# One half batch's x turned by VectorE and a scratch in DRAM instead of TensorE, with new order lists, in a fused attention and MLP kernel

## The chip, the cores and the metric

The kernel runs on one core of a Trainium2 chip. The metric is the time of one execution on the device in microseconds; the median of several runs counts. The engines are named as in the profile: PE (TensorE, matrix products), DVE (VectorE), ACT (ScalarE), POOL (GpSimd) and SP (SyncE, which issues most DMAs).

## The reference, cut to what matters

Attention over chosen chunks of keys for 4 batches, 8 heads, 768 positions and 64 dimensions a head, and then an MLP with ELU over all 3072 positions.

```python
top_chunks = np.argsort(ub, axis=-1)[..., -top_k:]     # 6 of 24 chunks of 32 keys, causal
scores = scale * np.matmul(q, k.transpose(0, 1, 3, 2))
...
scores = np.where(sel & causal, scores, -1e9)
attn = softmax(scores)
x = matmul(attn, v)            # to [3072, 512], heads side by side
h = x @ w_in                   # [3072, 2048]
g = np.where(h > 0, h, np.exp(np.minimum(h, 0)) - 1)
out = g @ w_out                # [3072, 512]
```

## The kernel before, in words

**Units.** A "pair" u (0 to 15) is two heads of a batch; batch b has pairs 4b to 4b+3. Each pair's queries are worked on in two halves of 384 positions (hf 0 and 1). "12,0" below is pair 12, first half; "half 3,0" is the MLP of batch 3's first half.

**Attention of a half pair** (`pair_attend`). PE makes the scores (line 863) in pieces, ACT takes their exponentials (L890), PE multiplies them with V (L922, six groups of matmuls, one for each of two heads and three blocks of 128 queries, "P·V" below), DVE takes the reciprocal of the sums (L935) and scales (L938), which gives the tile `on`: 128 positions on the partitions, three blocks of 128 features along the row. The MLP needs x with the features on the partitions, so PE turns `on` with three transposes into PSUM (L947), and ACT copies the result into `xT` (L950). An `xT` holds both halves of one pair, and one `up` of the MLP reads the `xT` of all four pairs of its batch.

**MLP of a half batch** (`mlp`). `up` (L972) makes 128 rows of h at a time (256 for batch 3, in a two-bank tile), ACT and DVE apply ELU (L982, L987, L990, L1000, L1005, L1011, L1016) and give `gT`; `down` (L1032) multiplies `gT` with `w_out`, in three row tiles of four parts; ACT copies to `osb` (L1041), and SP stores 128 rows of out (L1046).

**Buffers.** `caps` gives the number of buffers of each class. For what follows: `on` 3, `osb` 3, `f` 13 (loads of k, q, v, and the exponentials of ELU), `H` 3 (PSUM banks for `up` of batches 0 to 2, out of four single banks shared by all small PSUM tiles). A new tile of a class takes over a buffer and waits until all that read the old tile are done with it.

**What sets the order.** The operations are collected first with `add`, which numbers them in the order of the calls. For each engine `QUEUE` lists those numbers in the order in which that engine is to run them. `Plan.order` goes through the lists with its own estimates of durations and of the DMA rings and decides, by the time at which it believes a buffer to be free, which buffer a tile gets; it never changes the order of an engine. An engine runs its list strictly in order, so a waiting operation holds up all behind it. `free=[...]` names the buffers that an operation gives back, in the planner's reckoning after its `dur` plus `lat`. A `fetch` is a number of DMAs that SP issues, with 0.533 us of issue for each, `lat=0.0`, and a `DMA` operation that stands for the landing.

Of the kernel before, what the change touches and what calls it, by code (L numbers as in the profile page):

```python
# [14 lines left out]
BF16 = mybir.dt.bfloat16  # L15
# [58 lines left out]
    ],  # L74
    "POOL": [
# [10 lines left out]
    ],  # L86
    "ACT": [
# [20 lines left out]
    ],  # L108
# [5 lines left out]
    ],  # L114
# [43 lines left out]
class Plan:  # L158
# [71 lines left out]
    SHARE = {128: 1.0, 256: 0.35, 512: 0.3, 768: 0.3, 1024: 0.3, 2048: 0.5}  # L230
    HEAVY = 0.088
    RAMP = 240.0
    PAUSE = ((0.0, 2.28), (17.2, 17.8), (21.6, 22.4), (30.5, 31.3))
    LANDED = 0.75

    def served(self, rings, t, until):
# [877 lines left out]
```

## Time and profile before

| | |
|---|---|
| median of three runs | 273.88 us (272.23 to 274.41) |
| the profiled execution's own time | 273.46 us |
| its span, first to last instruction | 271.8 us, granted clock 0.998 |
| PE busy | 258.6 us, 95% |
| DVE, ACT, POOL busy | 206.8, 200.0, 118.3 us |
| the first load lands, PE starts | 4.2 us after the start |
| last matmul to the end of the span | 3.4 us |

How to read it: the busy share of an engine is an average over stages with different limits, and matmuls overlap in the profile, so their mean duration is more than what each adds; distances between starts show that. "A <- B" in a list of waits means that A's engine stood idle until B was done. In the timeline a row gives the start, the length from the first start to the last end of so many like instructions, engine, line, operation, what is written and read, and in brackets the idle time before. "SPq" is SP's queue of DMA issues.

### The profile page before, as it was taken

To read this page: it belongs to the slowest core of one execution; us is meant where nothing else is said; L and a number is where in the kernel's file an instruction comes from. 1 tells how busy PE (TensorE), PEld (TensorE's weight loads), DVE (VectorE), ACT (ScalarE), POOL (GpSimd) and SP (SyncE) were. 2 spreads that over 40 slices of the span, in tenths; PEclk is the share of its full clock that TensorE was granted. 3 is DMA by queue.
4 is the path that set the end of the run, shared out by engine and by line. 5 is a ranking of instruction groups with operands and counts; after the bars stand their busy time and mean duration, and the time that the engine had idled before them with its cause. 6 is when DMAs were issued, how large, how long until landed. Compare 5 with 4: busy or idle time off the path is not lost.

```text
span 271.8 us, 6603 instructions
## 1 busy us (share of the span) xinstructions
PE 258.6 (95%) x2456; PEld 160.0 (59%) x2456; DVE 206.8 (76%) x532; ACT 200.0 (74%) x375; POOL 118.3 (44%) x209
## 2 busy tenths in 40 slices
PE   3898899999999899999999999999999999999995
PEld 3787566655565455655565556665666655555544
DVE  5698979899999979889998867786666875137530
ACT  3899999846996589989899478977898744243512
POOL 3577783155876696870874055544330000000000
PEclk9999999999999999999999999999999999999999
DMA  7997999999999995999931010000210101110113
GB/s 218 266 211 124 205 216 214 164 176 151 148 203 130 192 169 115 139 156 201 240 103 41 1 58 22 0 2 3 76 41 1 41 2 39 39 41 0 65 53 116
DMA packets 112624, 29.79 MB, mean 110 GB/s; under 512 B 101200, under 2 KB 109648, under 8 KB 112592
## 3 DMA queue, kind: packets, MB, share of 16 engines
q1 hardware_dynamic: 107280, 24.39, 48.5%
q0 software_dynamic: 4224, 4.19, 9.3%
q10 hardware_dynamic: 1088, 0.79, 0.9%
q8 instruction: 19, 0.31, 0.5%
q14 instruction: 13, 0.11, 0.1%
HBM read 27.26 MB, written 6.29 MB: 123 GB/s over the span
## 4 chain that ended last, share of the span: by engine, by line
PE 78%; ACT 7%; DVE 6%; DMA 6%; issue 1%; SPq 1%; POOL 0%; DVEq 0%; ACTq 0%; POOLq 0%
PE psH L972 20%; PE psM L1032 20%; PE psS L863 10%; PE psS L972 8%; PE psMT L1032 8%; PE psO L922 6%; ACT pt L890 3%; DMA w_in_sb<-in_moe_w_in_dram 3%; PE psS L771 2%; ACT lhs L695 2%; PE psT L947 2%; DMA out_dram<-osb 1%; PE psMT L685 1%; DMA gT<-in_k_dram 1%; PE psH L685 1%
## 5 line engine op out<-in xcount | busy, mean ns | idle before, releaser
L890 ACT ACTIVATE pt<-psS 128x768 bf16<-128x768 f32 (+1 forms) x120 | 89.8, 781 | 11.3 <-PE psS L863 6.7
L972 PE MATMUL psH<-xT,w_in_sb 128*128 128x384 bf16 x384 | 73.7, 326 | 0.5 <-DMA w_in_sb<-in_moe_w_in_dram 0.4
L1032 PE MATMUL psM<-w_out_sb,gT 128*128 128x512 bf16 x288 | 72.1, 379 | 0.0
L972 PEld LDWEIGHTS <-w_in_sb 128*128 128x128 bf16 x512 | 47.7, 97 | 33.1 <-issue 1.3
L863 PE MATMUL psS<-rhs,lhs 88*128 88x384 bf16 (+4 forms) x304 | 54.6, 283 | 2.8 <-ACT pt L890 2.8
L1032 PEld LDWEIGHTS <-gT 128*128 128x128 bf16 x400 | 37.3, 97 | 33.0 <-DVE gT L1016 0.5
L982 ACT ACTIVATE f<-psH 128x384 f32<-128x384 f32 x96 | 47.0, 506 | 7.0 <-PE psH L972 6.1
L909 POOL TENSOR_SCALAR_AFFINE_SELECT pt<-pt 128x512 bf16<-128x512 bf16 (+1 forms) x48 | 24.7, 522 | 61.6 <-ACT pt L890 58.1
L1011 DVE SCALAR_TENSOR_TENSOR t<-f,psH 128x384 bf16<-128x384 f32 x56 | 30.1, 547 | 12.9 <-ACT f L982 12.4
L863 PEld LDWEIGHTS <-lhs 88*128 88x128 bf16 x304 | 27.4, 98 | 17.8 <-issue 3.0
L737 POOL CAST rhs<-f 64x768 bf16<-64x768 f32 (+1 forms) x40 | 27.7, 698 | 20.4 <-DVE f L622 8.6
L821 POOL COPY rhs<-selt 24x576 bf16<-24x576 bf16 (+2 forms) x40 | 22.7, 566 | 24.2 <-DVE selt L810 22.5
L922 PEld LDWEIGHTS <-pt 128*128 128x128 bf16 x672 | 28.3, 98 | 7.4 <-issue 1.0
L1016 DVE SCALAR_TENSOR_TENSOR gT<-psH,t 128x384 bf16<-128x384 f32 x56 | 30.5, 551 | 1.1
L922 PE MATMUL psO<-vext,pt 128*128 128x65 bf16 x672 | 31.1, 194 | 0.1
L950 ACT ACTIVATE xT<-psT 128x384 bf16<-128x384 bf16 x32 | 15.6, 497 | 11.9 <-PE psT L947 11.9
L972 PE MATMUL psS<-xT,w_in_sb 128*128 128x384 bf16 x128 | 22.9, 326 | 0.0
L982 ACT ACTIVATE f<-psS 128x768 f32<-128x768 f32 x16 | 13.0, 811 | 13.5 <-PE psS L972 13.5
L990 DVE SCALAR_TENSOR_TENSOR gT<-f,psH 128x384 bf16<-128x384 f32 x40 | 21.3, 541 | 2.0 <-ACT psH L987 1.3
L1032 PE MATMUL psMT<-w_out_sb,gT 128*128 128x512 bf16 (+1 forms) x112 | 22.6, 349 | 0.0
L737 POOL CAST lhs<-f 64x768 bf16<-64x768 f32 x24 | 19.7, 823 | 6.4 <-DVE f L604 5.5
L987 ACT ACTIVATE psH<-psH 128x384 f32<-128x384 f32 x40 | 20.2, 512 | 0.0
(55 smaller groups left out, 278.9 us busy)
## 6 DMA issues: line engine op xcount, KB each, us to landing
out_dram<-osb SPq DMA_DIRECT2D x23, 256.0 KB, 2.2
f<-in_k_dram SPq DMA_DIRECT2D x48, 96.0 KB, 3.9
f<-in_q_dram SPq DMA_DIRECT2D x48, 96.0 KB, 3.8
f<-in_v_dram SPq DMA_DIRECT2D x24, 192.0 KB, 3.9
w_in_sb<-in_moe_w_in_dram POOLq DMA_DIRECT2D x4, 512.0 KB, 9.2
w_out_sb<-in_moe_w_out_dram POOLq DMA_DIRECT2D x4, 512.0 KB, 14.7
gT<-in_k_dram SPq DMA_DIRECT2D x8, 192.0 KB, 4.3
gT<-in_v_dram SPq DMA_DIRECT2D x12, 128.0 KB, 4.2
```

The source lines that it names most:

```text
L737: nc.gpsimd.tensor_copy(out=o, in_=i)
L821: eng.tensor_copy(out=dst.rearrange("c h (i two x) -> c h i two x", two=2, x=32)[:, :, :, odd, :], in_=tiles[st][r0:r0 + NCH, c0:c0 + n].r ...
L863: nc.tensor.matmul(p_s[:, hd, pc:pc + w], lhsT=tiles[pt_["kb"]][0:64 + NCH, hd, 128 * kb:128 * kb + 128], rhs=tiles[pt_["qb"]][0:64 + NCH, ...
L890: lambda bs=bs, pt=pt, wtot=wtot, lo=lo, at=at: nc.scalar.activation(out=tiles[pt][:, :, lo:lo + wtot], in_=tiles[bs[0]][:, :, at:at + wto ...
L909: nc.gpsimd.affine_select(out=a, in_=a, compare_op=AOT.is_ge, fill=0.0, base=0, pattern=pat, channel_multiplier=-1)
L922: nc.tensor.matmul(po[:, hd, qi, :], lhsT=tiles[pt][:, hd, off:off + 128], rhs=tiles[pt_["vx"]][:, 6 * hd + kb, :], start=(kb == 0), stop= ...
L972: nc.tensor.matmul(ph, lhsT=w_in_sb[:, kk, f0:f0 + 128], rhs=tiles[XT[4 * b + kk]][:, c0:c0 + HALF], start=(kk == 0), stop=(kk == NKK - 1))
L982: lambda e=e, view=view: nc.scalar.activation(out=halves(e)[:, 0:step], in_=view(), func=AF.Exp),
L990: lambda e=e, view=view, fc=fc, gt=gt: nc.vector.scalar_tensor_tensor(out=tiles[gt][:, fc:fc + step, :], in0=halves(e)[:, 0:step], scalar= ...
L1011: lambda e=e, t=t, view=view: nc.vector.scalar_tensor_tensor(out=tiles[t][:, 0:step], in0=halves(e)[:, 0:step], scalar=1.0, in1=view(), op ...
L1016: lambda t=t, view=view, fc=fc, gt=gt: nc.vector.scalar_tensor_tensor(out=tiles[gt][:, fc:fc + step, :], in0=view(), scalar=0.0, in1=tiles ...
L1032: nc.tensor.matmul(pm, lhsT=tiles[gt][:, fc, 128 * tt:128 * tt + 128], rhs=w_out_sb[:, fc, x0:x1], start=(fc == 0), stop=(fc == NFC - 1))
```

## The change

For batch 3's first half alone (`TURN = ((3, 0),)`), that is for 12,0, 13,0, 14,0 and 15,0:

- The three transposes on PE, the PSUM bank for them and ACT's copy go. Instead DVE transposes `on` in blocks of 32x32 into a second buffer of class `on`; SP issues four stores of it into a scratch in DRAM (128 pieces of 192 bytes each), waits until they have landed, and issues one load of 128 rows of 768 bytes into `xT`. The operations in the lists are called the block transpose, the stores (PUT) and the load back (GET) below. The positions of the half then stand in another order along `xT`.
- Therefore out of that half is stored with two DMAs for a row tile instead of one, each to its own rows.
- Each of the four half pairs has 7 operations in place of 4, so there are 1671 instead of 1659, and numbers from 1405 on are shifted.
- Constants of the planner are changed, and all lists are new.

```diff
+    PAUSE = ((0.0, 2.28), (17.2, 18.0), (21.8, 22.6), (30.5, 31.3), (53.0, 54.0), (61.0, 62.0), (67.0, 68.2), ...
-        add("DMA", 0.0, -20.0, lambda: None, reads=[("asked", i)], writes=[name], lat=plan.LANDED)
+        add("DMA", 0.0, -20.0, lambda: None, reads=[("asked", i)], writes=[name], lat=plan.LANDED + (0.8 if i else 0.3))
...
+    TURN = ((3, 0),)
...
+            if (u // 4, hf) in TURN:
+                xb, = new("on")
+                there = dram.tile([P, HALF], BF16, name=f"xd{u}_{hf}")
...
+                def blocks():
+                    nc.vector.transpose(out=flat(xb).rearrange("p (j t x) -> p t j x", j=4, x=32),
+                                        in_=flat(on).rearrange("p (t j x) -> p t j x", j=4, x=32))
+                def put():
+                    for i in range(4):
+                        nc.sync.dma_start(out=there[:, 96 * i:96 * i + 96].rearrange("(j a) y -> a j y", j=4),
+                                          in_=flat(xb)[32 * i:32 * i + 32].rearrange("a (j y) -> a j y", j=4))
+                add("DVE", dve(HALF), pr, blocks, reads=[on], writes=[xb], alloc=[xb], free=[on])
+                fetch(4, 128, 192, pr, put, [("put", u, hf)], more=[xb], free=[xb])
+                fetch(1, 128, 768, pr,
+                      lambda: nc.sync.dma_start(out=tiles[xt_h][:, HALF * hf:HALF * hf + HALF], in_=there[:, :]),
+                      [(xt_h, hf)], more=[("put", u, hf)], alloc=[] if hf else [xt_h])
+                return
...
+                    if (b, hf) in TURN:
+                        def put(osb=osb, row=b * S + HALF * hf, tt=tt, x0=x0, x1=x1):
...
+                                nc.sync.dma_start(out=o4[i, t0:t0 + n],
+                                                  in_=tiles[osb][p0:p0 + 32 * n, 0:x1 - x0])
+                        add("SP", 1.066, pr, put, reads=[osb], free=[osb], move=(0, 1.08, 0.533, 2, 64, 4 * w))
```

The new lists around this place, with the numbers put into names (`sc` a score piece of two matmuls of 384 columns or as much, `up 2,1:4` the rows 128*4 on of half 2,1, `down 2,1 t1.0` row tile 1, part 0):

```
PE, before, 498 entries ahead of up 3,0:0; the last of them:
  P·V 15,0 (with transposes 14,0 in between), down 2,0 t2.3, sc 15,1, transposes 15,0, up 2,1:4, up 2,1:12, up 3,0:0
PE, after, also 498 entries ahead:
  P·V 14,0, sc 14,1, sc 14,1, transposes 12,1, down 2,0 t2.0, down 2,0 t2.1, P·V 15,0,
  up 2,1:4, down 2,0 t2.2, sc 14,1, up 2,1:14, down 2,0 t2.3, sc 15,1, up 2,1:3, sc 15,1,
  up 2,1:12, up 2,1:5, sc 14,1, up 2,1:13, down 2,1 t1.0, up 3,0:0, up 3,0:2, ...
  (transposes 13,1 follow 24 entries after up 3,0:0)
DVE, after:
  normalize 13,0, block transpose 13,0, ELU 2,1:2, ELU 2,1:9, normalize 13,1, ELU 2,1:10,
  normalize 14,0, block transpose 14,0, normalize 15,0, block transpose 15,0,
  ELU 2,1:4 (two operations), :11 (two), :14 (two), :3 (two), :12 (two), :5 (one), ELU 3,0:0, ...
SP, after:
  PUT 12, out 1,1 t2, GET 12, out 2,0 t0, PUT 13, PUT 14, out 2,0 t1, PUT 15, GET 14, GET 13, GET 15, out 2,0 t2, ...
```

Elsewhere the lists differ all along: the middle entry of a list is moved by 2 places (PE 3), nine entries in ten by no more than 5 to 9. At the start SP asks for the first halves' k of all four pairs one after the other, and POOL asks for the fourth piece of `w_in` behind a cast of pair 4, the V cast of 0,1 and a mask of chunks, where it stood ahead of these three. In SP's list out 0,0 t2 stands ahead of the k load of pair 11 instead of behind it.

More of the change, by code (lines that the diff above doesn't have):

```diff
@@ L227, in clocked @@
         return dur if warm else dur + dur
-    ALONE = {128: 0.0138, 256: 0.0188, 512: 0.036, 768: 0.0368, 1024: 0.055, 2048: 0.085}
-    SHARE = {128: 1.0, 256: 0.35, 512: 0.3, 768: 0.3, 1024: 0.3, 2048: 0.5}
+    ALONE = {128: 0.0138, 192: 0.0166, 256: 0.0188, 512: 0.036, 768: 0.0376, 1024: 0.055, 2048: 0.085}
+    SHARE = {128: 1.0, 192: 0.6, 256: 0.35, 512: 0.3, 768: 0.3, 1024: 0.3, 2048: 0.5}
     HEAVY = 0.088
     RAMP = 240.0
-    PAUSE = ((0.0, 2.28), (17.2, 17.8), (21.6, 22.4), (30.5, 31.3))
+    PAUSE = ((0.0, 2.28), (17.2, 18.0), (21.8, 22.6), (30.5, 31.3), (53.0, 54.0), (61.0, 62.0), (67.0, 68.2), (80.6, 81.6), (85.4, 86.2), (98.0, 99.0), (108.0, 109.0), (117.0, 118.0))
     LANDED = 0.75
@@ L257, in served @@
             if heavy and heavy[0][4]:
-                heavy[0][1] += self.RAMP
+                heavy[0][0] = t + self.RAMP * self.HEAVY / 16
                 heavy[0][4] = 0
+                continue
             rate = {}
@@ L269, in served @@
                     rate[e] = 16 / cyc
+            if not heavy and len(heads) == 2:
+                (e0, h0), (e1, h1) = heads
+                c0, c1 = self.ALONE[h0[2]], self.ALONE[h1[2]]
+                if max(c0, c1) > 1.5 * min(c0, c1):
+                    rate[e0] = 16 / c0 * (0.75 if c0 < c1 else 0.25)
+                    rate[e1] = 16 / c1 * (0.75 if c1 < c0 else 0.25)
             first = min(heads, key=lambda x: x[1][1] / rate[x[0]])
@@ L409 @@
     work = ctx.enter_context(tc.tile_pool(name="work", bufs=1))
+    dram = ctx.enter_context(tc.tile_pool(name="dram", bufs=1, space=bass.MemoryType.DRAM))
     psum = ctx.enter_context(tc.tile_pool(name="psum", bufs=1, space=bass.MemoryType.PSUM))
@@ L574, in fetch @@
         add(eng, 0.533 * starts, pr, f, reads=more, writes=[w] + writes, lat=0.0,
-            move=(0 if eng == "SP" else 1, 1.08 if eng == "SP" else 1.3, 0.533, starts, packets, size), **kw)
+            move=(0 if eng == "SP" else 1, 1.08 if eng == "SP" else 1.75, 0.533, starts, packets, size), **kw)
         add("DMA", 0.0, pr, lambda: None, reads=[w], writes=writes, lat=plan.LANDED)
+    TURN = ((3, 0),)
     PAIR = {}
@@ L941, in pair_attend, with flat @@
                 reads=o_all + [rc], writes=[on], alloc=[on], free=bo + [rc])
+            if (u // 4, hf) in TURN:
+                xb, = new("on")
+                there = dram.tile([P, HALF], BF16, name=f"xd{u}_{hf}")
+                def flat(h):
+                    return tiles[h].rearrange("p q h d -> p (q h d)")
+                def blocks():
[11 more added lines that the diff above has]
+                return
             bx = bank("T")
@@ L1044, in mlp @@
                     row = b * S + HALF * hf + 128 * tt
+                    if (b, hf) in TURN:
+                        def put(osb=osb, row=b * S + HALF * hf, tt=tt, x0=x0, x1=x1):
+                            o4 = out[row:row + HALF, x0:x1].rearrange("(t i r) y -> i t r y", i=4, r=32)
+                            for p0, i, t0, n in (((0, 0, 0, 3), (96, 1, 0, 1)), ((0, 1, 1, 2), (64, 2, 0, 2)),
+                                                 ((0, 2, 2, 1), (32, 3, 0, 3)))[tt]:
+                                nc.sync.dma_start(out=o4[i, t0:t0 + n],
+                                                  in_=tiles[osb][p0:p0 + 32 * n, 0:x1 - x0])
+                        add("SP", 1.066, pr, put, reads=[osb], free=[osb], move=(0, 1.08, 0.533, 2, 64, 4 * w))
+                        continue
                     add("SP", 0.533, pr,
```

171 rows, old and new, of the table QUEUE are left out of this document.

## Prediction

> **What bounds the kernel now.** I read the page first (shares, slices, chain), then the busy time by stretch, then who TensorE (PE) waited for, and last the timeline around the place of the change.
>
> ```profile
> span 271.8 us, 6603 instructions
> PE 258.6 (95%) x2456; PEld 160.0 (59%) x2456; DVE 206.8 (76%) x532; ACT 200.0 (74%) x375; POOL 118.3 (44%) x209
> PE   3898899999999899999999999999999999999995
> GB/s 218 266 211 124 205 216 214 164 176 151 148 203 130 192 169 115 139 156 201 240 103 41 1 58 22 0 2 3 76 41 1 41 2 39 39 41 0 65 53 116
> ```
>
> ```profile
> core 0: us, PE busy (x) PEld busy (x) DVE busy (x) ACT busy (x) POOL busy (x), PEclk, DMA share, GB/s
> 122.00:258.00 136.00, 136.00 (x1131) 80.08 (x1129) 95.73 (x216) 96.51 (x175) 37.83 (x63) 1.00 0.19 51
> 176.00:212.00 36.00, 36.00 (x370) 22.61 (x369) 23.68 (x67) 30.14 (x55) 11.81 (x21) 1.00 0.06 23
> ```
>
> ```profile
> engine line waited for: us in total, times, longest us
> PE psH L685 <- DMA gT<-in_k_dram: 4.2, 1, 4.2
> PE psS L863 <- ACT pt L890: 2.8, 5, 1.4
> PE psH L685 <- ACT qa L721: 1.1, 2, 0.9
> PE psT L947 <- DVE on L938: 0.8, 1, 0.8
> PE psH L972 <- DMA w_in_sb<-in_moe_w_in_dram: 0.4, 1, 0.4
> ```
>
> PE is the bound. From 122 to 258 us it is never idle, and the change lies inside that stretch: work taken off PE there shortens the kernel, and every wait put there lengthens it one for one. Outside it PE loses 4.2 us before the first load and 5.1 us (2.8 + 1.1 + 0.8 + 0.4) to single waits. VectorE (DVE) and ScalarE (ACT) are two thirds and five sixths busy around 176 to 212, and the transfers are at 23 GB/s there, against over 200 early on.
>
> **The change part by part.** (1) PE loses the twelve transposes of line 947 for pairs 12 to 15, first half; ACT loses four copies of line 950; DVE gains four block transposes.
>
> ```profile
> L947 PE MATMUL psT<-ident_b,on 128*128 128x128 bf16 x96 | 10.3, 219 | 0.9 <-DVE on L938 0.8
> L950 ACT ACTIVATE xT<-psT 128x384 bf16<-128x384 bf16 x32 | 15.6, 497 | 11.9 <-PE psT L947 11.9
> L810 DVE STREAM_TRANSPOSE selt<-selv 128x384 bf16<-128x384 bf16 x2 | 1.2, 578 | 0.0
> ```
>
> ```profile
> 208.16 0.35 PE L922 MATMUL psO<-vext,pt 128*128 128x65 bf16 x6
> 208.35 1.03 PE L1032 MATMUL psM<-w_out_sb,gT 128*128 128x512 bf16 x4
> 208.67 0.19 DVE L935 RECIPROCAL rc<-psO 128x6 f32<-128x6 f32 x1
> 208.89 0.56 DVE L938 TENSOR_TENSOR on<-psO,rc 128x384 bf16<-128x384 f32 x1
> 209.22 0.49 PE L863 MATMUL psS<-rhs,lhs 88*128 88x384 bf16 x2
> 209.54 0.33 PE L947 MATMUL psT<-ident_b,on 128*128 128x128 bf16 x3
> 209.71 1.46 PE L972 MATMUL psH<-xT,w_in_sb 128*128 128x384 bf16 x8
> 211.01 0.65 PE L972 MATMUL psS<-xT,w_in_sb 128*128 128x384 bf16 x3
> ```
>
> The mean of 219 ns is no price, because matmuls overlap. The distance from one start to the next is: three transposes 209.54 to 209.71, 0.17 us; an `up` of the earlier half 0.65 (two from 209.71 to 211.01); a `down` 0.87; a score piece 0.32; six P·V matmuls 0.19, so a pair's twelve take 0.38. Four times 0.17 is **-0.67 us** on PE's path. The ACT copies gain nothing, ACT not being the bound there. DVE's four block transposes (the same shape and type as line 810's row, 0.58 us each, 2.3 us) hide beside PE, DVE being busy 23.68 of 36 us; without that cover they would cost up to 2.3.
>
> (2) The round trip. Sixteen small stores (192-byte pieces) and four loads go through SP, which sits idle there, and the stores of out for half 3,0 go from three to six, three more issues of about 0.5 us beside this row:
>
> ```profile
> 189.32 79.95 SPq L1046 DMA_DIRECT2D out_dram<-osb  x14
> ...
> 0.81 1.97 SPq L663 DMA_DIRECT2D gT<-in_k_dram  x4
> ...
> DMA to landing us min/median/max: 2.0/2.0/2.7
> out_dram<-osb SPq DMA_DIRECT2D x2, 128.0 KB, 1.7
> ...
> DMA to landing us min/median/max: 2.5/3.8/17.8
> ```
>
> (Issues from 186 us on, four issues in a row, the landing of line 1046's stores between 186 and 212 us, the two 128 KB stores, the landing of line 592's 96 KB loads.) Four issues take 1.97 us, so the fourth starts 1.5 after the first. A landing x lies between 1.7 (the smallest store; ours have 24 KB) and 2.5 (the quickest load); I take 1.7 for a store, 2.0 for the load back.
>
> I put the new lists into names and time them with the distances above, from T, the end of pair 14's P·V. Pair 15's P·V ends at T+2.9 (two score pieces 0.64, the three transposes of 12,1 0.17, two `down` 1.74, its own 0.38). Then come six `up` 3.90, three `down` 2.61 and four score pieces 1.28 before the first `up` of half 3,0: due at T+10.7. It needs all four pairs. Normalizing ends 1.1 after P·V (208.35 to 209.45), the block transpose 0.6 later: pair 14's at T+1.7. Its stores are issued at once and land at T+3.2+x.
>
> Here is what I expect to go wrong. The class `on` has three buffers. When pair 15's block transpose is to start, one holds 13,1 (its PE transposes stand behind `up` of half 3,0), one holds pair 15's own normalized tile, and one pair 14's turned tile, which four stores are still reading. The planner frees that after its four issues (2.13 us, `lat=0.0`); the chip must wait for the landing, as ACT does for a store of out in the row at 93.39 below. So pair 15's block transpose starts at T+3.2+x instead of T+4.0: it waits x-0.8, 0.9 us at x=1.7. Behind it in DVE's list stand the eleven operations for `up` 4, 11, 14, 3, 12 and 5 of half 2,1.
>
> ```profile
> L1011 DVE SCALAR_TENSOR_TENSOR t<-f,psH 128x384 bf16<-128x384 f32 x56 | 30.1, 547 | 12.9 <-ACT f L982 12.4
> L1016 DVE SCALAR_TENSOR_TENSOR gT<-psH,t 128x384 bf16<-128x384 f32 x56 | 30.5, 551 | 1.1
> ```
>
> Each pair of them takes 1.1 us and frees one of three `H` banks; `up` 3, 12, 5 and 13 each need one. Followed through in turn, `up` 13 starts some 0.15 less late than the block transpose did: PE loses **0.8 us**. The transfers alone give T+3.8+x for the end of the block transpose, T+5.3+2x for its stores, T+5.3+3x for the load back, against T+10.7: a stall of 3x-5.4, nothing at 1.7, 0.6 at 2.0, 2.1 at 2.5. These two waits overlap. Ends of the term: 0 (the planner's own spacing, 0.15 in hand at the buffer) and 2.1; I stay near the store rows, since nothing else moves then. Pair 14's normalizing takes the buffer of pair 13's turned tile in the same way, but its P·V comes 4.9 us after pair 13's: 0.3 us in hand at x=2.
>
> The Trainium skill ("DMA: Bandwidth & Descriptors", section "Anatomy of one DMA — SWDGE (gpsimd) path") gives a DMA of GpSimd's path a fixed cost of about 2.0 us, most of it the receipt of the write, and warns that it is longest towards HBM. If SP's path is alike, x would be 2.0 for stores too, the wait 1.2 and the loss 1.05, so the sum would end 0.25 higher; the trace has 1.7 for 128 KB and 2.0 for 256 KB, and I keep the rows.
>
> (3) The lists made anew. The planner's constants emit nothing; they only move buffers. One place in the lists can be priced, here from the chain of waits and the timeline:
>
> ```profile
> 87.76 0.52 SPq L592
> ...
> 88.33 0.82 SPq L592
> ...
> 89.19 0.59 SPq L592
> ...
> 89.82 3.55 DMA out_dram<-osb
> ```
>
> ```profile
> 93.39 0.60 ACT L1041 ACTIVATE osb<-psM 128x512 f32<-128x512 f32 x1 [1.74 <-DMA out_dram<-osb]
> 94.74 0.49 PE L863 MATMUL psS<-rhs,lhs 88*128 88x384 bf16 x2 [1.36 <-ACT pt L890]
> 95.44 0.48 PE L863 MATMUL psS<-rhs,lhs 88*128 88x384 bf16 x2 [0.22 <-ACT pt L890]
> ```
>
> ACT waits 1.74 us for a store of out that frees its buffer, and PE 1.58 us for ACT. In SP's new list that store stands ahead of pair 11's k load, whose four issues it stood behind: it can go about 2 us earlier (89.82 less 87.76), more than the 1.74, so the wait could go whole. But what holds SP there are free `f` buffers, and ACT's list around it is another too. Ends 0 and -1.6; I take half, **-0.8 us**. The other 3.5 us of single waits (5.1 less 1.6) lie before 36 us and around 75, where the new lists load the first halves' k first and ask for the fourth weight piece later; with nothing to size that by, I take 0, with ends -3.5 and, for new waits of the sizes seen, +4.
>
> Sum: 273.46 - 0.67 + 0.8 - 0.8 = 272.8 us for the profiled execution (its span of 271.8 and 1.7 around it). The median of the three runs is 0.42 above that execution, and what will be measured is a median, so I predict **273.2 us**. One per cent, 271.1 to 276.6, is about what a measurement of this kernel can tell from no change: three runs of before lie 2.2 us apart.
>
> **The rivals.** Rival 1, the trip is hidden and the lists are better: the buffer comes free in time, PE gains the whole 0.67, and the wait at 94.74 goes whole: 273.88 - 0.67 - 1.58 = 271.6; with a third of the other 3.5 us gone as well, 270.4. For it speaks the planner's spacing, which has left PE without a gap since 95.44 us in before; against it, the buffer is free in time only up to x = 0.8, and no store row is under 1.7.
>
> Rival 2, on the slower side: the trip itself becomes the bound, at the first `up` of half 3,0. With landings as on a loaded queue (x = 3.8, line 592's median) the stall is 3x-5.4 = 6.0 us: 273.88 - 0.67 - 0.8 + 6.0 = 278.4. It decides (above 276.6) from a stall of 4.2, that is from x = 3.2. For it speaks that the load reads just what was stored and that the pieces are small; against it the quiet stretch (23 GB/s, stores at 2.0). Such a stall would bring a second price, seen at the start:
>
> ```profile
> 4.21 1.51 PE L685 MATMUL psH<-ident_f,gT 128*128 128x128 f32 x6 [4.21 <-DMA gT<-in_k_dram]
> 12.47 0.82 PE L685 MATMUL psH<-ident_f,gT 128*128 128x128 f32 x6
> ```
>
> After 4.2 us without work PE's six transposes took 1.51 us instead of 0.82, at a granted clock of 1.00; after the 1.36 at 94.74 nothing was slower. By the Trainium skill ("TensorE: Matmul & The Clock Gate", the table of the two states) PE falls to half speed after an idle window of about 3.4 us and needs as long to recover; that would add about 1.7 us, so 280.1. The trace agrees at its start and shows no such gap later.
>
> Rival 3, new waits elsewhere: order lists fitted to one trace meet other transfer times. Each wait of before past the start costs PE at most 1.4 us; two new ones make 273.2 + 2.8 = 276.0, four 278.8. For it speaks that nearly every list is changed in the early, loaded stretch; against it that most entries moved by a few places only.
>
> **How the numbers follow.** My forecast has a chance of 0.55, with 271.2 to 275.2 as its own range (the trip's term from 0 to 2.1, the wait at 94.74 from -1.6 to 0, and about 1 us either way for the rest); rival 1 0.20, rival 2 0.08, rival 3 0.17. The range 270.3 to 277.0 takes in the forecast, nearly all of rival 1 and half of rival 3, and leaves out rival 2 and the rest. Faster by over 1%: 0.13, over half of rival 1 and a little of the forecast. Slower by over 1%: 0.19, rival 2, over half of rival 3 and a little of the forecast. Within 1%: 0.68.
>
> **What would show it.** Line 947 has 84 transposes instead of 96 and line 950 28 copies. The block transpose of pair 15 starts at the landing of pair 14's stores, not at the end of its normalizing, some 0.9 us late; PE then shows gaps of together about 0.8 us at line 972 between pair 15's P·V and the first `up` of half 3,0, named for DVE or for the load. Four stores take 3.2 us from first issue to last landing, the load back 2.0. The wait at 94.74 is gone or smaller. I am wrong if PE has no gap there (then the buffer is freed earlier than I think), if one of several us stands there (rival 2), or if the time moves before 100 us instead (rival 3, or 1).

## The result and the profile after

The changed kernel takes 271.19 us (median of 10 runs), the kernel before 273.58 us beside it; the ratio is 0.9925, 95% interval [0.9898, 0.9951]. A second measurement (after_again below) gave 271.9 beside 273.54 us, 0.994 [0.9915, 0.9965]. So it is 0.6 to 0.8% faster, 1.3 to 2.0 us below the forecast of 273.2 and inside the range of 270.3 to 277.0. The profiled execution took 272.74 us, one of the longer ones; most spans are 269 to 269.6.

The page of the kernel after, and its busy time in the stretch in which PE was never idle before (columns as shown there: length, then PE, PEld, DVE, ACT, POOL):

```profile
span 271.0 us, 6628 instructions
PE 257.2 (95%) x2417; PEld 159.9 (59%) x2444; DVE 207.0 (76%) x536; ACT 199.4 (74%) x371; POOL 118.4 (44%) x209
L981 ACT ACTIVATE xT<-psT 128x384 bf16<-128x384 bf16 x28 | 13.6, 500 | 7.7 <-PE psT L978 7.5
L978 PE MATMUL psT<-ident_b,on 128*128 128x128 bf16 x84 | 9.1, 219 | 0.5 <-DVE on L948 0.4
```

```profile
122.00:258.00 136.00, 134.95 (x1115) 79.39 (x1129) 94.65 (x208) 94.18 (x168) 38.04 (x63) 1.00 0.26 59
```

PE is still the bound. It has 84 transposes and ACT 28 copies, as announced (27 records of matmuls of `down` are missing in this trace, so part of the 1.05 us that PE seems idle from 122 to 258 us is no idle time; the timeline below shows what is).

The waits of PE:

```profile
PE psH L695 <- DMA gT<-in_k_dram: 4.5, 2, 4.2
PE psH L1003 <- DMA w_in_sb<-in_moe_w_in_dram: 1.7, 1, 1.7
PE psS L873 <- ACT pt L900: 0.8, 3, 0.4
PE psH L1003 <- DVE gT L1047: 0.8, 2, 0.5
...
PE psT L978 <- DVE on L948: 0.4, 1, 0.4
```

Set beside those of before: waits for other engines fall from 4.7 us (2.8 + 1.1 + 0.8) to 2.0 (0.8 + 0.8 + 0.4). The wait of 1.7 us for a piece of `w_in` belongs to this execution: it was 0.3 us in the second profile of the same kernel. `ACT qa`, 1.1 us in before, is gone.

The place of the change, DVE first, then SP's issues, then PE:

```profile
203.19 0.58 DVE L960 STREAM_TRANSPOSE on<-on 128x384 bf16<-128x384 bf16 x1
...
205.24 0.56 DVE L948 TENSOR_TENSOR on<-psO,rc 128x384 bf16<-128x384 f32 x1
206.76 0.58 DVE L960 STREAM_TRANSPOSE on<-on 128x384 bf16<-128x384 bf16 x1 [0.97 <-DMA xd<-on]
...
209.92 0.56 DVE L1047 SCALAR_TENSOR_TENSOR gT<-psH,t 128x384 bf16<-128x384 f32 x1
```

```profile
207.37 1.73 SPq L965 DMA_DIRECT2D xd<-on  x4
209.26 1.40 SPq L970 DMA_DIRECT2D xT<-xd  x3
...
xT<-xd SPq DMA_DIRECT2D x3, 96.0 KB, 2.1
xd<-on SPq DMA_DIRECT2D x10, 24.0 KB, 1.6
```

```profile
189.31 0.81 PE L1003 MATMUL psH<-xT,w_in_sb 128*128 128x384 bf16 x4
...
209.47 0.81 PE L1003 MATMUL psH<-xT,w_in_sb 128*128 128x384 bf16 x4
210.53 0.82 PE L1003 MATMUL psH<-xT,w_in_sb 128*128 128x384 bf16 x4 [0.25 <-DVE gT L1047]
...
213.04 2.28 PE L1003 MATMUL psS<-xT,w_in_sb 128*128 128x384 bf16 x13
```

(The two rows of SP's transfers between 200 and 212 us end with the median time to landing.) The wait foretold is there: pair 15's block transpose stands 0.97 us for the landing of pair 14's stores. Behind it the third ELU result that frees an `H` bank, the one of `up` 14, is done at 210.48 (209.92 + 0.56), and `up` 5, which stands right behind `up` 12 in PE's list, starts 1.06 after it instead of 0.65. PE loses 0.41 us there, counted from start to start; the bracket has the 0.25 of it that lie behind the end of the matmuls before. The first `up` of half 3,0, at 213.04, waits for nothing. (The row at 189.31 is `up` 1 of half 2,1, from which a stretch is measured below.)

### The profile page after: what moved, and what is told of

Its sections match the earlier page's. It is cut to its first block, busy times and chain, and to the rows that moved or that the text cites. A ratio compares the mean times of both kernels' runs of the same rounds, so it can differ in the third digit from the quotient of the medians.

```text
span 271.0 us, 6628 instructions
## 1 busy us (share of the span) xinstructions
PE 257.2 (95%) x2417; PEld 159.9 (59%) x2444; DVE 207.0 (76%) x536; ACT 199.4 (74%) x371; POOL 118.4 (44%) x209
## 4 chain that ended last, share of the span: by engine, by line
PE 74%; DMA 9%; DVE 5%; ACT 4%; SPq 3%; issue 2%; ACTq 0%; POOL 0%; DVEq 0%
PE psH L1003 19%; PE psM L1063 18%; PE psS L873 10%; PE psS L1003 8%; PE psMT L1063 8%; PE psO L932 6%; DMA w_in_sb<-in_moe_w_in_dram 3%; PE psS L781 2%; DMA gT<-in_q_dram 2%; ACT pt L900 2%; DMA gT<-in_k_dram 2%; DMA f<-in_k_dram 1%; PE psT L978 1%; ACT f L1013 1%; DVE t L1042 1%
## 5 line engine op out<-in xcount | busy, mean ns | idle before, releaser
L900 ACT ACTIVATE pt<-psS 128x768 bf16<-128x768 f32 (+2 forms) x120 | 88.7, 777 | 7.9 <-PE psS L873 5.2
L1063 PE MATMUL psM<-w_out_sb,gT 128*128 128x512 bf16 x265 | 69.1, 379 | 1.2
L1063 PEld LDWEIGHTS <-gT 128*128 128x128 bf16 x400 | 37.9, 98 | 34.6 <-DVE t L1042 0.5
L919 POOL TENSOR_SCALAR_AFFINE_SELECT pt<-pt 128x256 bf16<-128x256 bf16 (+1 forms) x48 | 24.6, 522 | 66.3 <-ACT pt L900 65.4
L932 PEld LDWEIGHTS <-pt 128*128 128x128 bf16 x672 | 26.9, 98 | 5.1 <-POOL pt L919 0.3
L932 PE MATMUL psO<-vext,pt 128*128 128x65 bf16 x672 | 29.1, 193 | 0.0
L1063 PE MATMUL psMT<-w_out_sb,gT 128*128 128x512 bf16 (+1 forms) x108 | 21.9, 347 | 0.2
L981 ACT ACTIVATE xT<-psT 128x384 bf16<-128x384 bf16 x28 | 13.6, 500 | 7.7 <-PE psT L978 7.5
```

Source lines behind the costliest of these rows:

```text
L900: lambda bs=bs, pt=pt, wtot=wtot, lo=lo, at=at: nc.scalar.activation(out=tiles[pt][:, :, lo:lo + wtot], in_=tiles[bs[0]][:, :, at:at + wto ...
L919: nc.gpsimd.affine_select(out=a, in_=a, compare_op=AOT.is_ge, fill=0.0, base=0, pattern=pat, channel_multiplier=-1)
L932: nc.tensor.matmul(po[:, hd, qi, :], lhsT=tiles[pt][:, hd, off:off + 128], rhs=tiles[pt_["vx"]][:, 6 * hd + kb, :], start=(kb == 0), stop= ...
L1063: nc.tensor.matmul(pm, lhsT=tiles[gt][:, fc, 128 * tt:128 * tt + 128], rhs=w_out_sb[:, fc, x0:x1], start=(fc == 0), stop=(fc == NFC - 1))
```

## The experiments

All compute the same. The lists were edited by the names of the operations; before and after are the two kernels of this document.

**lists_alone: the new lists, without the turn.**

```diff
-    TURN = ((3, 0),)
+    TURN = ()
 QUEUE PE, after's:
+  transposes 12,0 behind up 2,1:1; 13,0 behind up 2,1:9; 14,0 behind down 2,0 t2.0; 15,0 behind down 2,0 t2.2
 (ACT's copies right behind in the same way)
```

> The new lists without the turn: the twelve transposes of line 947 and the four copies are back, at the places where their inputs are ready. Theory A (most of the gain is the new lists: PE loses less time ahead of 100 us; the turn itself gives 0.67 us and takes back 0.4): about 271.5 us, 2 us below before, and PE's lost time up to 100 us as in the changed kernel. Theory B (the gain is the turn: less work on PE and ACT, a PSUM bank less): 273.5 us, no gain.

Measured: 274.26 us beside 273.54, ratio 1.0022 [1.0007, 1.0036]; neither theory. PE's timeline shows why:

```profile
187.90 0.81 PE L1003 MATMUL psH<-xT,w_in_sb 128*128 128x384 bf16 x4
188.55 0.33 PE L978 MATMUL psT<-ident_b,on 128*128 128x128 bf16 x3
189.33 0.77 PE L932 MATMUL psO<-vext,pt 128*128 128x65 bf16 x19 [0.45 <-DVE gT L1047]
...
197.62 0.33 PE L978 MATMUL psT<-ident_b,on 128*128 128x128 bf16 x3
199.00 0.43 PE L932 MATMUL psO<-vext,pt 128*128 128x65 bf16 x8 [1.05 <-DVE gT L1047]
...
205.35 0.54 PE L932 MATMUL psO<-vext,pt 128*128 128x65 bf16 x12
206.25 0.81 PE L1003 MATMUL psH<-xT,w_in_sb 128*128 128x384 bf16 x4 [0.37 <-ACT xT L981]
...
207.93 0.49 PE L873 MATMUL psS<-rhs,lhs 88*128 88x384 bf16 x2
208.67 0.81 PE L1003 MATMUL psH<-xT,w_in_sb 128*128 128x384 bf16 x4 [0.25 <-ACT xT L981]
...
214.64 2.60 PE L1003 MATMUL psS<-xT,w_in_sb 128*128 128x384 bf16 x15
```

Measured from start to start, less what the first row costs when nothing waits (0.17, 0.17, 0.38, 0.33), PE loses 0.61 + 1.21 + 0.52 + 0.41 = 2.75 us at four places where after loses nothing. What P·V and `up` wait for is one of the four single PSUM banks (psO and psH are tiles in such banks): a transposed tile holds one from PE's transposes to ACT's copy. That reading was put to the test with bank_held.

The stretch from the start of `up` 1 of half 2,1 to that of the first `up` of half 3,0 has the same PE list in both kernels but for the twelve transposes. It takes 26.74 us here (187.90 to 214.64) and 23.73 in after (189.31 to 213.04; 23.73 in the second profile too). The difference of 3.01 is 2.75 and the transposes' 0.67, less the 0.41 that only after loses.

**bank_held: the bank without the work.** The version own_buffer (below), with one PE transpose and a short ACT copy at lists_alone's places.

```diff
+                bx = bank("T")
+                def one(on=on, bx=bx):
+                    nc.tensor.transpose(ps(bx, [P, HALF], BF16)[:, 0:128], tiles[on][:, 0, :, :], ident_b)
+                add("PE", 0.06, pr, one, reads=[on, "ident_b"], writes=[bx[0]], alloc=bx)
+                add("ACT", 0.25, pr, lambda bx=bx: nc.scalar.activation(out=spare[:, :],
+                    in_=ps(bx, None, None)[:, 0:32], func=AF.Copy), reads=[bx[0]], writes=[("spare", u)], free=bx)
                 return
```

> The version with the turned tile in a buffer of class qa, and for each of the four half pairs one PE transpose of 128 columns (not used) into a bank of class T and an ACT copy of 32 of its columns, at the places where the run of the new lists without the turn has its three transposes and its copy. The bank is held as there; PE's added work is 4 x 0.06 = 0.23 us and ACT's copies are short. Theory A (the new lists without the turn lost their time because P·V waits for one of the four shared banks, so the turn's second gain is the bank that it leaves free): waits of PE at P·V between 185 and 212 us come back, together 1 to 2 us, and the time is 271.8 to 272.8 us. Theory B (it was ACT's four copies of 0.5 us, or the transposes' own time): no such waits, 270.5 to 270.9 us.

Measured: 274.41 us beside 273.47, ratio 1.0028 [0.9999, 1.0057]. The waits of theory A are back at the same places:

```profile
189.36 0.22 PE L979 MATMUL psT<-ident_b,on 128*128 128x128 bf16 x1
190.49 0.77 PE L935 MATMUL psO<-vext,pt 128*128 128x65 bf16 x19 [0.91 <-DVE gT L1059]
...
198.78 0.22 PE L979 MATMUL psT<-ident_b,on 128*128 128x128 bf16 x1
200.02 0.41 PE L935 MATMUL psO<-vext,pt 128*128 128x65 bf16 x8 [1.02 <-ACT spare L982]
```

The last of them is named for the short copy itself. From start to start, less 0.06 for the one transpose, these two are 1.07 and 1.18, and two waits at `up` behind them 0.35 and 0.18: 2.8 us together, as in lists_alone, though PE's own work there is a third and ACT's copies are of 32 columns. So it is the bank, as theory A says. The stretch measured above takes 26.29 us here and 23.30 in both profiles of own_buffer: the difference of 2.99 is these waits and the 0.24 of added transposes. The time itself is above theory A's bound, 3.7 us over own_buffer's second measurement of 270.69. The 0.7 us not accounted for stay open: in the profiled execution they lie ahead of the stretch or behind it, and the first loads landed later there.

**store_first: before, with one entry of SP's list moved.**

```diff
 QUEUE SP, before's:
+  out 0,0 t2
   k load of pair 11
-  out 0,0 t2
```

> The kernel before with one entry moved: in SP's list the store of out 0,0 t2 stands ahead of pair 11's k load instead of behind it. Theory A (the four issues ahead of the store make ACT and PE wait at 94 us): the store issues about 2 us earlier, PE's 1.58 us at 94.7 shrink to under 0.5, 272.3 us. Theory B (free f buffers and ACT's own order hold that place): the wait stays or another takes its place, 273.5 us.

Measured: 272.11 us beside 273.54, ratio 0.9952 [0.9933, 0.9972], 1.43 us faster: theory A. ACT and PE at that place now:

```profile
92.99 0.59 ACT L1042 ACTIVATE osb<-psM 128x512 f32<-128x512 f32 x1
...
94.66 0.87 PE L864 MATMUL psS<-rhs,lhs 88*128 88x384 bf16 x4
95.37 1.89 PE L1033 MATMUL psM<-w_out_sb,gT 128*128 128x512 bf16 x8
```

The copy to `osb` has no wait for the store, and the score pieces follow each other without one.

**early_new, late_new, late_107, late_185: the new order in one part only.** early_new has after's order for all that the planner starts before 135 us, before's order behind it, and no turn. The three others have before's order up to 135, 107 and 185 us and after's, with the turn, behind it.

```diff
 QUEUE, each engine:
-  before's list
+  early_new: [n in after's list if planned start < 135] + [n in before's list otherwise], TURN = ()
+  late_X:    [n in before's list if planned start < X] + [n in after's list otherwise], TURN = ((3, 0),)
```

> The new order for all that the planner starts before 135 us, the old order behind that, no turned half batch. Theory A (the changed kernel's gain beyond the turned half comes from fewer waits in the first 100 us): PE has lost some 1 to 2 us less by 100 us than the 15.7 us of the kernel before, nothing is lost from 122 us on, and the time is 271.5 to 272.5 us beside 273.5 before. Theory B (the early waits are only displaced, and the gain comes from the stretch behind 135 us): 273.5 us, PE having lost as much as before at 135 us, or new gaps behind the seam.

> The old order up to 135 us of the planner's time, the new one with the turned half batch behind it. Theory A (the late part is worth only the twelve transposes less the wait at the up of half 3,0): 273.5 - 0.67 + 0.43 = 273.3 us, the wait of about 1.4 us near 94.7 us still there, and PE gaps of about 0.4 us between the P·V of 15,0 and the first up of half 3,0. Theory B (the gain lies in the late part): 271.5 to 272 us.

> As the run with the old order up to 135 us and the new order with the turned half behind it, but with the seam at 107 us, where PE, ACT, DVE and SP have the same work behind them in both orders. That takes away the 5.4 us of waits that stood at the seam at 142 to 152 us. Theory A (the late part is worth only the twelve transposes less the wait at the H banks): 273.5 - 0.67 + 0.43 = 273.3 us, the waits of 1.4 us near 94.7 us still there. Theory B (the gain lies in the late part): 271.5 to 272 us.

> The old order up to 185 us, the new order with the turned half behind it. Theory A (of the new order only the stretch around the turn is needed for the trip, the rest before it is worth nothing): 273.3 us, PE without a gap from 122 us to the turn, and gaps of together 0.4 us between the P·V of 15,0 and the first up of half 3,0. Theory B (the new order of the stretch from 107 to 185 us is needed too, for instance to have ELU done or buffers free when the turn comes): 274 us or more, with new gaps between 185 and 215 us.

Measured: early_new 272.17 beside 273.45 us, ratio 0.9957 [0.9937, 0.9977], theory A. late_new 278.8 us, ratio 1.0207 [1.0179, 1.0235], neither: the seam itself made waits.

```profile
142.74 0.81 PE L1004 MATMUL psH<-xT,w_in_sb 128*128 128x384 bf16 x4 [1.73 <-DVE gT L1022]
...
145.30 0.48 PE L874 MATMUL psS<-rhs,lhs 88*128 88x384 bf16 x2 [0.56 <-ACT pt L901]
...
148.50 0.48 PE L874 MATMUL psS<-rhs,lhs 88*128 88x384 bf16 x2 [1.41 <-ACT pt L901]
...
152.35 0.72 PE L782 MATMUL psS<-f,km 64*32 64x288 f32 x16 [1.69 <-ACT pt L901]
```

Without these 5.4 us it would be 273.4, but such a subtraction proves little. At 107 us PE, ACT, DVE and SP have the same work behind the seam in both orders, and late_107 took 273.04 us beside 273.47, ratio 0.9979 [0.9954, 1.0004]: theory A, with the 0.25 us wait at `up` 5 as in after; the wait near 94.7 us is there, though only 0.9 us (0.68 + 0.22) in its profiled execution. late_185 took 273.77, ratio 1.0 [0.9971, 1.0029]; theory A's 273.3 and theory B's 274 both lie in the interval (272.7 to 274.3), so the time decides nothing. Its trace shows a wait of 0.10 us at the seam and one of 0.25 at `up` 5 between 185 and 215 us, nearly as A says, so the order between 107 and 185 us is not needed for the trip.

**own_buffer, own_again: the turned tile in a class of its own.** The tile for the block transpose comes from class `qa`, whose buffers are idle by then.

```diff
-                xb, = new("on")
+                xb, = new("qa")
+                TURNED.add(xb)
...
-            shape, dt = ([P, 8, HALF], F32) if h in STAGED.values() else shapes[c]
+            shape, dt = ([P, 8, HALF], F32) if h in STAGED.values() else shapes["on"] if h in TURNED else shapes[c]
```

> The changed kernel, with the turned tile in buffers of class qa, which nothing else uses at that time, instead of class on. Theory A (the wait of 0.97 us of pair 15's block transpose for pair 14's stores is what costs PE its 0.42 us there): the block transpose of pair 15 starts within 0.1 us of its normalizing, the first up of half 3,0 comes 0.4 us earlier against pair 15's P.V, 270.8 us. Theory B (PE waits there for the load back or for DVE anyway): PE loses the same 0.4 us, 271.2 us.

Measured: 270.54 beside 273.54 us, ratio 0.9889 [0.9855, 0.9922], theory A; again, on another chip:

> The version with the turned tile in a buffer of class qa once more, because its first time (270.54 us) rests on few runs, and the run with the bank held came out some 1.5 us above that time plus its added work and waits. Theory A (the first time holds, and the 1.5 us belong to the run with the bank held): 270.4 to 271.0 us beside 273.5 before. Theory B (the first loads land later in some sessions than in others, for every kernel with the new early order): 271.5 to 272.5 us, with PE waiting 1 us or more for loads between 5 and 40 us.

Measured: 270.69 beside 273.7 us, ratio 0.9897 [0.9868, 0.9925]: theory A by the time. (Its profiled execution, at 271.8 the longest of the six, waits 1.5 us for loads between 5 and 40 us, which was the sign of theory B: how the first loads land differs from execution to execution.) This is the fastest version. DVE, then PE, in the first of the two:

```profile
203.44 0.56 DVE L949 TENSOR_TENSOR on<-psO,rc 128x384 bf16<-128x384 f32 x1
204.03 0.58 DVE L962 STREAM_TRANSPOSE qa<-on 128x384 bf16<-128x384 bf16 x1
...
207.19 0.56 DVE L1049 SCALAR_TENSOR_TENSOR gT<-psH,t 128x384 bf16<-128x384 f32 x1
```

```profile
207.67 1.46 PE L1005 MATMUL psH<-xT,w_in_sb 128*128 128x384 bf16 x8
```

The block transpose follows the normalizing at once, and `up` 5 follows `up` 12 (eight matmuls in one run, the second four at 208.32). The `H` bank was free at 207.75, so there were 0.57 us in hand. A delay of 0.97 less 0.57 is 0.40: what after loses. The stretch measured above takes 23.30 us in both profiles, 0.43 less than in after; the medians differ by more, 0.5 to 1.4 us, which the turn does not explain.

**extra_hop: a third transfer in the trip.** The changed kernel, with the scratch copied to a second scratch before the load back.

```diff
+                hop = dram.tile([P, HALF], BF16, name=f"xh{u}_{hf}")
+                def back():
+                    nc.sync.dma_start(out=tiles[xt_h][:, HALF * hf:HALF * hf + HALF], in_=hop[:, :])
+                def hopped():
+                    nc.sync.dma_start(out=hop[:, :], in_=there[:, :])
+                    BACK.append(back)
+                    if u in (12, 15):
+                        while BACK:
+                            BACK.pop(0)()
...
-                      lambda: nc.sync.dma_start(out=tiles[xt_h][:, HALF * hf:HALF * hf + HALF], in_=there[:, :]),
+                      hopped,
```

> The changed kernel with one step added to the trip: the stores' scratch is copied to a second scratch in DRAM, and the load back reads that. It adds a third transfer of about 2.1 us between the stores and the load back. Theory A (the trip has about 0.6 us in hand at the first up of half 3,0, which the landing of the load back sets from there on): PE loses about 1.5 us at that up, in place of nothing there, the waits at the H banks staying 0.4: 272.5 to 272.9 us beside 271.2 of the changed kernel. Theory B (several us are in hand, the trip is hidden): 271.2 us. Theory C (the trip is the bound already): 273.3 us or more.

Measured: 272.62 us beside 273.45, ratio 0.9974 [0.9948, 1.0001]: theory A.

```profile
212.51 0.48 PE L1014 MATMUL psS<-xT,w_in_sb 128*128 128x384 bf16 x2 [0.86 <-DMA xT<-xh]
213.49 2.27 PE L1014 MATMUL psS<-xT,w_in_sb 128*128 128x384 bf16 x13 [0.49 <-DMA xT<-xh]
...
xh<-xd SPq DMA_DIRECT2D x3, 96.0 KB, 2.3
```

The matmul at 213.49 is the first that reads pair 15's part of x. Set against the `up` that waits for its bank (at 208.82 here, at 210.53 in after), it starts 1.67 us later than in after, and the last load back lands 2.75 later (at 213.44, where after's is issued at 210.3 and lands 2.1 later). So that load had about 1.1 us in hand in the changed kernel.

**turn_old_lists: the turn in the lists of before.**

```diff
 QUEUE, before's:
-  transposes (PE) and copies (ACT) of 12,0 to 15,0
+  DVE: each block transpose right behind its normalizing
+  SP:  out 2,0 t0, PUT 12, GET 12, out 2,0 t1, PUT 13, GET 13, PUT 14, PUT 15, GET 14, GET 15
```

> The turned half put into the old lists: the block transpose right behind the normalizing, the stores and loads behind the stores of out 2,0. There the first up of half 3,0 stands right behind pair 15's P·V, so the trip is uncovered. Theory A: from P·V to the end of the load back it is 1.1 + 0.6 + 0.1 + 3.1 + 2.1 = 7.0 us with little on PE beside it, so PE stands still some 5 to 7 us, and if its clock falls after that as at the start (six transposes 0.7 us longer), some 1 to 3 us more: 278 to 283 us, with matmuls behind the gap longer than before. Theory B (other work in PE's list, the second halves' scores and the last up of half 2,1, covers it): under 275 us, that is, the new order was not needed for the trip. With no slower matmuls behind a gap of over 3.4 us the price is the gap alone.

Measured: 281.24 us beside 273.45, ratio 1.0298 [1.0267, 1.0329]: theory A. PE, and then its busy time and granted clock in short windows:

```profile
209.45 0.49 PE L1004 MATMUL psS<-xT,w_in_sb 128*128 128x384 bf16 x2
214.77 0.48 PE L1004 MATMUL psS<-xT,w_in_sb 128*128 128x384 bf16 x1 [4.83 <-DMA xT<-xd]
215.84 3.97 PE L1004 MATMUL psS<-xT,w_in_sb 128*128 128x384 bf16 x13 [0.59 <-DMA xT<-xd]
```

```profile
core 0: us, PE busy (x), PEclk, DMA share, GB/s
...
210.00:212.00 2.00, 0.00 (x0) 1.00 0.07 16
212.00:214.00 2.00, 0.00 (x0) 0.62 0.24 47
...
218.00:219.00 1.00, 1.00 (x5) 0.50 0.00 0
219.00:220.00 1.00, 1.00 (x7) 0.84 0.20 76
```

Uncovered, the trip costs 5.4 us of waiting. The thirteen matmuls behind it take 3.97 us instead of 2.28 (the same thirteen in after): 1.7 us more, the second price of rival 2. Together, less the 0.67 for the transposes, that is 6.4 of the 7.8 us; the rest was not followed up.

**after_again: the changed kernel again**, on the chip of lists_alone, store_first and own_buffer.

> The changed kernel once more, for a second trace: the profiled execution of it took 272.74 us, its median is 271.19. Theory A (the 1.7 us that PE waits at 36 us for w_in's second piece are that execution's alone): the wait is under 0.5 us here and the span about 269.4 us. Theory B (it is in every execution): 1.7 us again, and the missing 1.6 us differ somewhere else.

Measured: 271.9 us, ratio 0.994 [0.9915, 0.9965], and 0.3 us of waiting for the piece of `w_in`: theory A, though the span is 270.0 us and not 269.4. The waits for ELU that stand at 86.6, 88.7 and 210.5 us in the first profile are the same in both, those for first loads are not.

## Why the prediction came out as it did

The time is within 1% of before and in the range, and the mechanism foretold at the turn is there. The forecast was 1.3 to 2.0 us too high, for three reasons: the turn's wait was counted 0.4 too large, the new early order was priced too low by 0.5 to 1.2, and the kernel before runs at 273.5 to 273.7 on these chips and not at 273.88. That the time lies in the range owes something to the range's width: the forecast's own part of it, 271.2 to 275.2, is only just reached. And one term that is larger than all of these, the bank, was not seen at all; it does not show in the comparison of before and after, only in the runs that take the two parts of the change apart.

*Step 1, the transposes.* The 0.67 us of PE work are off, and the block transposes (0.58 us each) hide beside PE. But PE's time was not all that the turn returns: it also gives back a PSUM bank. In the new lists that is worth 2.75 us (lists_alone; bank_held shows the cause). Together, 0.67 + 2.75 less the 0.41 lost at `up` 5 is 3.0, which the traces have in the stretch of the turn; lists_alone less after is 2.4 by the medians of one chip (274.26 - 271.9) and 3.1 by after's first measurement (274.26 - 271.19). The prediction had no term for the bank, since PE has no such wait in the profile of before: its order kept the banks apart, and the new order does not. So the 2.75 us are what the turn saves within the new lists, and no gain over before.

*Step 2, the round trip.* The wait of the block transpose for a buffer whose stores have not landed was right in place, cause and size: 0.97 us for 0.9. What failed is "`up` 13 starts some 0.15 less late than the block transpose did": the `up` that waits is `up` 5, two entries earlier, and its bank had 0.57 us in hand, so the term is +0.41 instead of +0.8. own_buffer removes the wait and shows the slack. A part of the difference is in the price of ELU: the prediction counted 0.6 + 3 x 1.1 = 3.9 us from the start of the block transpose to the third result, and it was 3.72 (206.76 to 210.48). Four stores took 2.8 us from first issue to last landing (issues 1.73 long, landing 1.6 by the median) instead of 3.2, and the load back 2.1 instead of 2.0. The rule of the Trainium skill ("DMA: Bandwidth & Descriptors", section "Anatomy of one DMA — SWDGE (gpsimd) path") of about 2.0 us would have made the wait 1.2; here, on SP's path, it was 0.97, with 1.6 us for these stores.

*Step 3, the store of out.* store_first measures the term by itself: -1.43 us, nearly the whole of the end of -1.6 and not the half that was taken. In after the wait at 94.7 is gone, but waits of 0.53 and 0.14 us have come at 86.60 and 88.66 (the first is in `psH <- DVE gT` among the waits above), so by the idle times the place is worth about -0.9.

*The rest of the lists, taken as 0.* It is a gain. early_new, which contains the store's term, is worth -1.28, with a wait of 0.36 us at its own seam; in after's profile the waits for `ACT qa`, for `on` and for `pt` before 36 us are gone or halved. Set together, 273.5 - 1.3 - 0.67 + 0.41 is 271.9, the second measurement of the changed kernel; the first is 0.7 lower, and own_buffer, 0.9 below its sum of 271.5 (273.5 - 1.3 - 0.67), says that early_new gives the early part too low. lists_alone agrees: 0.72 above before with 2.75 us of new waits, it must have gained 2.0 elsewhere. The second profile of the changed kernel lies between: it reaches the first `up` of half 3,0 at 212.02, 1.01 us later than before (211.01), but with three `up` and one `down` more done by then and the twelve transposes less (+2.15 us of work), and with the 0.41 lost, so it had gained 1.55. The early order is therefore worth 1.3 to 2.0 us; how much of that is the loads landing at other times was not separated.

*The rivals.* The time lies in rival 1's range (270.4 to 271.6) or just above it: its half on the lists came true, its half on the trip did not, for the trip was not hidden. Rival 2 does not happen in the changed kernel, 1.1 us short of it by extra_hop; in the old lists it does, with both its prices. The row read for the second price was a weak sign: at the start of before the granted clock reads 1.00 while the six transposes take 1.51 us, so that row does not show that the clock slowed them; turn_old_lists, with 0.50, does. Of rival 3 there are the 0.53 and 0.14 us.

## What to carry to other kernels

When a tile is moved off an engine, price the memory that it no longer holds (here a PSUM bank, 2.75 us) as well as the engine's time (0.67 us); a trace without a wait for that memory says only that the present order avoids it. A buffer that a store reads came free here at the landing and not after the issue: give such a tile a buffer of a class with room, which was worth some 0.4 us here for a small edit. And when an order is made anew, undo it alone, and cut two orders only where each engine has the same work behind the seam; of the two cuts at 135 us one cost 5.4 us and the other 0.36. Where medians of single sessions lie 0.7 us apart, measure the same stretch of the traces: here two profiles of one kernel agreed to 0.01 us.

## What was not expected of the hardware

PE's clock after a gap, in turn_old_lists: PE had no work from 209.9 us on (the last row before the gap, 209.45 + 0.49), and the granted clock of 0.62 over 212 to 214 us means that it fell to 0.50 near 212.5, after 2.6 us. PE worked without a break from 215.84 on and had the full clock back near 219.3 (0.84 over 219 to 220 us), 3.5 us later. The table of the two states in the Trainium skill ("TensorE: Matmul & The Clock Gate", Part 1) has about 3.4 us for both; the way back agrees, the fall came sooner, and the measurement decides. The same page of the Trainium skill says that its window runs freely. Fall and return lie 6.8 us apart here, which is two such windows; then the window that ended with the fall began near 209.1, and PE worked in its first 0.8 us. That would fit a window which counts as idle though not empty, but one gap does not show it.

Some transfers of half 3,0's out, where a row tile is stored in two pieces, took long, though nothing waits for them (between 236 and 262 us, after):

```profile
out_dram<-osb SPq DMA_DIRECT2D x2, 256.0 KB, 2.0
...
out_dram<-osb SPq DMA_DIRECT2D x2, 64.0 KB, 5.2
```

The two pieces of 64 KB landed after 5.2 us by the median, two whole row tiles after 2.0; for the other pieces, of 128 and 192 KB, the view has no time. Why is open.
